# A long convolution by FFT with a routed MLP: padded input blocks, a wider last stage and a reordered first transform

## The chip, the cores and the metric

One Trainium2 chip, one core of it. The metric is the device time of one launch in microseconds (us). Engines: PE multiplies matrices, DVE (VectorE), ACT (ScalarE) and POOL (GpSimd) work on vectors, SP issues most transfers. The kernel before takes 1100.68 us, the median of 3 runs (1099.55 to 1101.87).

## The reference

The convolution of x (8 batches, 6336 positions, 128 channels) with h along the sequence, then for each batch an MLP on the 128 positions with the highest score:

```python
def _attn_ref(x, h):
    L = 2 * S
    Xf = np.fft.rfft(x, n=L, axis=1)
    Hf = np.fft.rfft(h, n=L, axis=0)
    y = np.fft.irfft(Xf * Hf[None, :, :], n=L, axis=1)[:, :S, :]
    return y

def _moe_ref(x, w_gate, w1, w2, capacity):
    scores = np.einsum('bsd,d->bs', x, w_gate)
    out = x.copy()
    for b in range(B):
        top_idx = np.argpartition(-scores[b], capacity)[:capacity]
        xe = x[b, top_idx]
        ye = np.maximum(xe @ w1, 0.0) @ w2
        g = 1.0 / (1.0 + np.exp(-scores[b, top_idx]))
        out[b, top_idx] = x[b, top_idx] + g[:, None] * ye
    return out
```

All inputs are float32; capacity is 128.

## The kernel before, in words

The sequence is written as 99 n1 by 64 n2 (6336 = 99 x 64). Two batches are worked on at once, so there are four groups g. For one group and one half of the channels (u is 0 or 1) the work has four stages.

- **stage_a** transforms over n1. The host lays the input out folded around the middle of n1 (`_lay`), in eight blocks of eight channels. `load` (L83) brings a block into one of two slots of the big tile `slots`, 64 + 50 = 114 partitions by 1024 numbers. `turn` (L158) makes the sum and the difference of its halves on DVE (tile `xs`, L164), up to three blocks ahead. For each block PE then makes two units of matmuls (L186), and each unit's PSUM tile is emptied by ACT, one in eight by DVE (L190, through the helper at L67 and L69).
- **stage_b** goes through 25 chunks of up to four k1. `over_n2` (L228) multiplies by a table `wb` (matmuls at L63), lets ACT make a swapped copy in PSUM (L234, L235), multiplies by the spectrum of h on DVE (twice L239) and adds the two products on POOL (L246). Each chunk needs a table and a piece of spectrum, 256 KB each. `stage_first` does the same for the first u of group 0 and makes the spectrum of h on the way, which it stores to `hd`.
- **stage_c** transforms over k2 with the constant table `wc`: 16 units, each 16 matmuls and one copy of 99 x 1024.
- **stage_d** goes over the 64 n2, two per step (`nd` = 2). Four matmuls of 256 columns fill half of a PSUM tile `both` of 1024 columns that two steps share; ACT copies the half to `hr` (L283) and issues the output DMA (L285); POOL multiplies by `w_gate` (L288; DVE does it for the last step of the last two pairs), and DVE reduces to scores (L291). Its tables come in pairs of n2, half of them into `hr`.

The selection of the 128 positions (`pick`) is one generator with 26 steps of small DVE operations and small matmuls, and the MLP (`feed`) another; `mix` (L485) takes a step of the side work after every so many steps of the main work, at given rates. The schedule is manual: each engine runs its instructions in the order in which the code issues them. In group 0 the order is four units of stage_c, then stage_a for x's second half with one unit of stage_c after every fourth, then the second stage_b. In later groups both halves of stage_a come first, with the selection of the group before at rate 0.1, then both stage_b, the second with stage_c of the first half beside it. The eight loads of a half of x are issued one after another on SP; those of group 0's second half go out in the last eight chunks of stage_first. PSUM has four tiles of 1024 columns, used in turn. The tag `t` of six tiles serves `xs`, the products `tx` and the gated copy `tm`.

## Time and profile before

| | |
|---|---|
| median of 3 runs | 1100.68 us |
| profiled execution, its own time | 1103.47 us |
| its span | 1101.7 us |
| PE busy | 919.0 us (83%) |
| DVE busy | 653.4 us (59%) |
| ACT busy | 566.3 us (51%) |
| POOL busy | 427.3 us (39%) |
| DMA | 194.75 MB, 177 GB/s mean over the span |

The profile is of one execution. Its busy shares are means over stages that differ in what limits them, and PE's busy time is modelled, since matmuls are pipelined. Matmuls of float32 stand as two instructions each in the trace. The granted clock is that of PE as a share of 2.4 GHz; 0.50 is the lower of its two levels, 1.2 GHz.

### The profile page before, as it was taken

To read this page: it belongs to the slowest core of one execution; us is meant where nothing else is said; L and a number is where in the kernel's file an instruction comes from. 1 tells how busy PE (TensorE), PEld (TensorE's weight loads), DVE (VectorE), ACT (ScalarE), POOL (GpSimd) and SP (SyncE) were. 2 spreads that over 40 slices of the span, in tenths; PEclk is the share of its full clock that TensorE was granted. 3 is DMA by queue.
4 is the path that set the end of the run, shared out by engine and by line. 5 is a ranking of instruction groups with operands and counts; after the bars stand their busy time and mean duration, and the time that the engine had idled before them with its cause. 6 is when DMAs were issued, how large, how long until landed. Compare 5 with 4: busy or idle time off the path is not lost.

```text
span 1101.7 us, 34992 instructions
## 1 busy us (share of the span) xinstructions
PE 919.0 (83%) x14710; PEld 787.8 (72%) x14710; DVE 653.4 (59%) x1250; ACT 566.3 (51%) x845; POOL 427.3 (39%) x340
## 2 busy tenths in 40 slices
PE   6899798788878799988878799988868799888765
PEld 5699787775567589865577699855667699755544
DVE  3456556402365879644576878735667787544573
ACT  4477576542247777532277676522466776422101
POOL 0034315405530875035504765045406853055301
PEclk9799999998998999999999899999999999999888
DMA  3578659665536996425458885345368972055100
GB/s 146 178 236 255 226 151 245 198 192 178 162 121 215 335 306 194 156 84 159 129 177 266 276 284 173 112 123 162 123 203 274 307 252 78 14 158 152 57 5 10
DMA packets 115195, 194.75 MB, mean 177 GB/s; under 512 B 11344, under 2 KB 54224, under 8 KB 115040
## 3 DMA queue, kind: packets, MB, share of 16 engines
q1 hardware_dynamic: 87776, 165.52, 47.4%
q10 hardware_dynamic: 26752, 25.96, 7.1%
q8 instruction: 117, 1.92, 0.7%
q0 software_dynamic: 512, 1.05, 0.3%
q14 instruction: 38, 0.31, 0.1%
HBM read 156.27 MB, written 39.45 MB: 178 GB/s over the span
## 4 chain that ended last, share of the span: by engine, by line
PE 42%; DVE 9%; issue 5%; DMA 5%; ACT 4%; POOL 4%; SPq 0%; POOLq 0%; ACTq 0%; DVEq 0%
PE p L63 25%; PE p L279 10%; PE p L186 4%; DMA w<-tab_wb 4%; POOL tm L288 3%; ACT hr L283 2%; DVE tx L239 1%; DVE cmp L321 1%; DVE num L324 1%; DVE xs L164 1%; PE m L63 1%; ACT p L234 1%; DVE sc L291 1%; ACT p L235 1%; DVE slots L239 1%
## 5 line engine op out<-in xcount | busy, mean ns | idle before, releaser
L246 POOL TENSOR_TENSOR slots<-slots,tx 128x512 f32<-128x512 f32 (+1 forms) x200 | 255.7, 1298 | 344.1 <-DVE tx L239 256.5
L67 ACT COPY slots<-p 99x1024 f32<-99x1024 f32 (+3 forms) x266 | 247.7, 935 | 166.1 <-PE p L63 86.5
L63 PE MATMUL p<-wc,slots 128*64 128x128 f32 (+1 forms) x4096 | 248.0, 276 | 9.9 <-POOL slots L246 8.9
L288 POOL TENSOR_TENSOR tm<-hr,wg 99x512 f32<-99x512 f32 x120 | 155.4, 1299 | 255.8 <-ACT hr L283 199.6
L63 PEld LDWEIGHTS p<-wc,slots 128*64 128x64 f32 (+1 forms) x4096 | 229.5, 127 | 13.5 <-POOL slots L246 10.2
L63 PE MATMUL p<-slots,w 128*64 128x128 f32 (+1 forms) x2900 | 200.6, 283 | 40.2 <-DMA w<-tab_wb 19.5
L63 PEld LDWEIGHTS p<-slots,w 128*64 128x64 f32 x2900 | 172.9, 138 | 55.9 <-ACT p L235 35.1
L291 DVE TENSOR_REDUCE sc<-tm 99x4 f32<-99x512 f32 x128 | 87.5, 685 | 207.5 <-POOL tm L288 207.2
L283 ACT COPY hr<-p 99x512 f32<-99x512 f32 x128 | 74.9, 585 | 222.9 <-PE p L279 175.1
L279 PE MATMUL p<-slots,hr 99*99 99x256 f32 x512 | 128.3, 391 | 50.0 <-ACT hr L283 50.0
L186 PE MATMUL p<-fx,xs 50*64 50x99 f32 x4608 | 133.2, 266 | 43.1 <-issue 22.5
L186 PEld LDWEIGHTS p<-fx,xs 50*64 50x64 f32 x4608 | 119.8, 146 | 56.7 <-issue 29.3
L239 DVE TENSOR_TENSOR slots<-p,hr 128x512 f32<-128x512 f32 (+1 forms) x175 | 119.3, 682 | 63.2 <-ACT p L235 61.6
L279 PEld LDWEIGHTS p<-slots,hr 99*99 99x99 f32 x512 | 79.4, 165 | 98.5 <-ACT hr L283 77.3
L234 ACT ACTIVATE p<-p 64x512 f32<-64x512 f32 (+1 forms) x200 | 113.1, 566 | 56.8 <-PE p L63 47.0
L279 PE MATMUL p<-slots,w 99*99 99x256 f32 x512 | 123.0, 381 | 4.6 <-ACT slots L67 4.6
L164 DVE TENSOR_TENSOR xs<-slots 114x512 f32<-114x512 f32 x144 | 94.3, 707 | 50.0 <-PE p L186 26.2
L239 DVE TENSOR_TENSOR tx<-p,hr 128x512 f32<-128x512 f32 (+1 forms) x175 | 118.0, 674 | 0.0
L235 ACT COPY p<-p 64x512 f32<-64x512 f32 (+1 forms) x200 | 110.8, 554 | 6.3
L279 PEld LDWEIGHTS p<-slots,w 99*99 99x99 f32 x512 | 82.8, 164 | 32.1 <-ACT slots L67 5.6
L69 DVE COPY slots<-p 99x1024 f32<-99x1024 f32 (+2 forms) x54 | 48.8, 904 | 34.6 <-ACT slots L67 25.7
L63 PE MATMUL p<-slots 128*64 128x64 f32 (+1 forms) x664 | 47.1, 249 | 3.5 <-ACT p L234 3.5
(90 smaller groups left out, 516.1 us busy)
## 6 DMA issues: line engine op xcount, KB each, us to landing
w<-tab_wb SPq DMA_DIRECT2D x172, 256.0 KB
hr<-hd SPq DMA_DIRECT2D x144, 256.0 KB
slots<-in_x SPq DMA_DIRECT2D x64, 456.0 KB
out<-hr ACTq DMA_DIRECT2D x128, 198.0 KB
w<-tab_at SPq DMA_DIRECT2D x64, 153.1 KB
hr<-tab_at SPq DMA_DIRECT2D x64, 153.1 KB
hr<-hd SPq DMA_DIRECT2D x48, 128.0 KB
slots<-tab_wb SPq DMA_DIRECT2D x20, 256.0 KB
```

Of the source, the lines that this page charges most:

```text
L63: nc.tensor.matmul(out[a:b], table[:, a:b], moving, start=start, stop=stop)
L67: nc.scalar.copy(out=dst, in_=src)
L164: v.tensor_tensor(out=xt[0:HX].rearrange("p d n -> p (d n)"), in0=flat[0:HX, o:o + XB // 2], in1=flat[0:HX, o + XB // 2:o + XB], op=op)
L186: nc.tensor.matmul(pt[c * 64:(c + 1) * 64, o:o + N1], xt[c][e, q * 4 + j], fx[e, c * N1:(c + 1) * N1], start=True, stop=True)
L234: nc.scalar.mul(out=pw[0:64], in_=pv[64:128], mul=-1.0)
L235: nc.scalar.copy(out=pw[64:128], in_=pv[0:64])
L239: v.tensor_tensor(out=dst, in0=src.rearrange("p k (b j t) -> p k b j t", b=2, t=2), in1=ht[:, t, 0:kn].rearrange("p k (j t) -> p k j t", t ...
L246: adds.tensor_tensor(out=yv, in0=yv, in1=tx.rearrange("p k (j t) -> p k j t", t=2), op=ALU.add)
L279: nc.tensor.matmul(pt[0:N1, i * 2 * D:(i + 1) * 2 * D], at[:, i % 2, c], zp[:, :, c * N2 + m], start=(c == 0), stop=(c == 1))
L283: nc.scalar.copy(out=yt.rearrange("p b n (u d) -> p (n u) b d", u=2), in_=pt[0:N1, 0:512].rearrange("p (n b d) -> p n b d", b=nb, d=HD))
L288: (v if m0 in (N2 - 6, N2 - 2) else nc.gpsimd).tensor_tensor(out=tm, in0=hr[0:N1, o:o + 512].rearrange("p (c d) -> p c d", d=D), in1=wg[0: ...
L291: v.tensor_reduce(out=ss[:, :, m0:m0 + nd], in_=tm.rearrange("p (b n) d -> p b n d", b=nb), axis=AX.X, op=ALU.add)
```

## The change

Four things. The host no longer cuts the zero rows off the input, and `load` brings 128 partitions instead of 114; `turn` still reads 114. stage_d takes four n2 per step: each step has a PSUM tile of its own, one ACT copy and one output DMA of twice the size, and the gating product and its reduction go batch by batch, each still of 512 numbers; DVE multiplies the second batch of the last two steps. In groups 1 to 3 the second half of stage_a stands beside the first stage_b, 0.7 of its units after each chunk, and the MLP's rate there is 0.36 instead of 0.4; the selection is taken along at rate 0.1 in the first half of stage_a only. In group 0 four units of stage_a come ahead of all of stage_c, then one unit of stage_c after every second, and x's second half is requested four chunks earlier in stage_first.

```diff
     def load(src, u, blocks=range(8)):
         for i in blocks:
-            nc.sync.dma_start(out=flat[0:HX, u * XS + i * XB:u * XS + (i + 1) * XB], in_=src[i])
+            nc.sync.dma_start(out=flat[:, u * XS + i * XB:u * XS + (i + 1) * XB], in_=src[i])
...
-        nb, nd = 2, 2
+        nb, nd = 2, 4
...
-            if m0 % (2 * nd) == 0:
-                both = banks()
-            pt = both[:, m0 % (2 * nd) * 2 * D:]
+            pt = banks()[0:N1]
...
-            o = m0 // nd % 4 * 512
-            yt = hr[0:N1, o:o + 512].rearrange("p (b n d) -> p b n d", b=nb, d=D)
+            o = m0 // nd % 2 * 1024
+            yt = hr[0:N1, o:o + 1024].rearrange("p (b n d) -> p b n d", b=nb, d=D)
             nc.scalar.copy(out=yt.rearrange("p b n (u d) -> p (n u) b d", u=2),
-                           in_=pt[0:N1, 0:512].rearrange("p (n b d) -> p n b d", b=nb, d=HD))
+                           in_=pt.rearrange("p (n b d) -> p n b d", b=nb, d=HD))
             nc.scalar.dma_start(out=ov[:, :, m0:m0 + nd], in_=yt)
-            tm = tp.tile([N1, 4, D], F32, tag="t", name="tm", bufs=6)
-
-            (v if m0 in (N2 - 6, N2 - 2) else nc.gpsimd).tensor_tensor(
-                out=tm, in0=hr[0:N1, o:o + 512].rearrange("p (c d) -> p c d", d=D),
-                in1=wg[0:N1].unsqueeze(1).broadcast_to([N1, 4, D]), op=ALU.mult)
-            v.tensor_reduce(out=ss[:, :, m0:m0 + nd], in_=tm.rearrange("p (b n) d -> p b n d", b=nb),
-                            axis=AX.X, op=ALU.add)
-            if m0 % (2 * nd):
-                yield
+            for b in range(nb):
+                tm = tp.tile([N1, nd, D], F32, tag="t", name="tm", bufs=6)
+
+                (v if b and m0 >= N2 - 2 * nd else nc.gpsimd).tensor_tensor(
+                    out=tm, in0=yt[:, b], in1=wg[0:N1].unsqueeze(1).broadcast_to([N1, nd, D]), op=ALU.mult)
+                v.tensor_reduce(out=ss[:, b, m0:m0 + nd], in_=tm, axis=AX.X, op=ALU.add)
+            yield
...
     for i, _ in enumerate(stage_first()):
-        if i >= NK - 8:
-            load(x[0, 1], 0, [i - NK + 8])
+        if NK - 12 <= i < NK - 4:
+            load(x[0, 1], 0, [i - NK + 12])
...
         if g:
-            mix(itertools.chain(stage_a(0, 0, [(1, 0), (1, 8)]), stage_a(1, D)), (side, 0.1))
-            mix(stage_b(g, 0), (iter(()) if g < 2 else fed.pop(0), 0.4))
+            mix(stage_a(0, 0, [(1, 0), (1, 8)]), (side, 0.1))
+            a = stage_a(1, D)
+            mix(stage_b(g, 0), (iter(()) if g < 2 else fed.pop(0), 0.36), (a, 0.7))
+            rest(a)
         else:
-            mix(itertools.islice(c, 4))
-            mix(stage_a(0, D), (c, 0.25))
+            a = stage_a(0, D)
+            rest(itertools.islice(a, 4))
+            mix(a, (c, 0.5))
...
-    r = r.reshape(a.shape[:-5] + (128, XB))
-    return r[..., :HX, :]
+    return r.reshape(a.shape[:-5] + (128, XB))
```

The order of the instructions on PE in stage_d, with what each waits for (DMAHW is a landing, Activation is ACT, PE is PE itself). Before, a step of two n2 takes one table, `w` or `hr` in turn:

```order
L279 MATMUL p<-slots,w 99x256 [waits DMAHW6_49,PE_49]
L279 MATMUL p<-slots,w 99x256 x3
L279 MATMUL p<-slots,hr 99x256 [waits DMAHW0_49,Activation_49]
L279 MATMUL p<-slots,hr 99x256 x3
L279 MATMUL p<-slots,w 99x256 [waits DMAHW2_49,PE_49]
L279 MATMUL p<-slots,w 99x256 x3
L279 MATMUL p<-slots,hr 99x256 [waits DMAHW4_49,Activation_49]
L279 MATMUL p<-slots,hr 99x256 x3
```

and of the change:

```order
L277 MATMUL p<-slots,w 99x256 [waits DMAHW4_49,Activation_49]
L277 MATMUL p<-slots,w 99x256 x3
L277 MATMUL p<-slots,hr 99x256 [waits DMAHW5_49]
L277 MATMUL p<-slots,hr 99x256 x3
L277 MATMUL p<-slots,w 99x256 [waits DMAHW7_49,Activation_49]
L277 MATMUL p<-slots,w 99x256 x3
L277 MATMUL p<-slots,hr 99x256 [waits DMAHW0_49]
L277 MATMUL p<-slots,hr 99x256 x3
```

The wait for ACT has moved from the second half of four n2, whose PSUM tile ACT is reading at that time, to the first, where it is for the copy of the tile that was filled four tiles earlier.

PE from the end of stage_d in group 0 on, with L186 stage_a (16 matmuls a unit), L63 from `slots,w` the first products over n2 (8 matmuls a chunk). Before:

```order
L279 MATMUL p<-slots,hr 99x256 x4
L186 MATMUL p<-fx,xs 64x99 x512
L63 MATMUL p<-slots,w 64x128 x238
L63 MATMUL p<-wc,slots 64x128
L63 MATMUL p<-wc,slots 35x128
```

and of the change:

```order
L277 MATMUL p<-slots,hr 99x256 x4
L186 MATMUL p<-fx,xs 64x99 x256
L63 MATMUL p<-slots,w 64x128 x16
L186 MATMUL p<-fx,xs 64x99 x16
L63 MATMUL p<-slots,w 64x128 x8
L186 MATMUL p<-fx,xs 64x99 x16
L63 MATMUL p<-slots,w 64x128 x16
L186 MATMUL p<-fx,xs 64x99 x16
```

The second 256 matmuls of stage_a now come in units of 16 behind every first or second chunk.

DVE at the end of stage_d in group 1, where L408 and L404 (`hit`) and what follows are the last operations of the selection of group 0, L392 and L388 its lane operations, L164 the turns for group 2. Before:

```order
L394 SCALAR_TENSOR_TENSOR cmp<-tri,first,cmp 99x128
L291 TENSOR_REDUCE sc<-tm 99x2x2 x4
L408 TENSOR_SCALAR hit<-m,cst 128x256
...
L291 TENSOR_REDUCE sc<-tm 99x2x2 x2
L164 TENSOR_TENSOR xs<-slots 114x512 x4
L291 TENSOR_REDUCE sc<-tm 99x2x2 x3
L288 TENSOR_TENSOR tm<-hr,wg 99x512
L291 TENSOR_REDUCE sc<-tm 99x2x2 x2
L288 TENSOR_TENSOR tm<-hr,wg 99x512
L291 TENSOR_REDUCE sc<-tm 99x2x2
L164 TENSOR_TENSOR xs<-slots 114x512 x8
```

and of the change:

```order
L164 TENSOR_TENSOR xs<-slots 114x512 x4
L289 TENSOR_REDUCE sc<-tm 99x4 x3
L287 TENSOR_TENSOR tm<-hr,wg 99x512
L289 TENSOR_REDUCE sc<-tm 99x4
L388 TENSOR_SCALAR cmp<-tri,last 99x128
L390 SCALAR_TENSOR_TENSOR cmp<-tri,first,cmp 99x128
L388 TENSOR_SCALAR cmp<-tri,last 99x128
L390 SCALAR_TENSOR_TENSOR cmp<-tri,first,cmp 99x128
L289 TENSOR_REDUCE sc<-tm 99x4
L287 TENSOR_TENSOR tm<-hr,wg 99x512
L289 TENSOR_REDUCE sc<-tm 99x4
L404 TENSOR_SCALAR hit<-m,cst 128x256
```

The selection, which ended before the turns of the next group's first two blocks, now ends behind the last reduction; the turns of the third block come after it.

## Rows read from the trace of the kernel before

**Rows 1.** Timeline of the opening: start us, us, engine, line, operation, idle before and releaser.
```profile
6.51 1.29 DVE L164 TENSOR_TENSOR xs<-slots 114x512 f32<-114x512 f32 x2 [5.50 <-DMA slots<-in_h]
9.47 1.29 DVE L164 TENSOR_TENSOR xs<-slots 114x512 f32<-114x512 f32 x2 [1.67 <-DMA slots<-in_h]
...
40.09 3.42 PE L186 MATMUL p<-fx,xs 50*64 50x99 f32 x64 [0.90 <-DVE xs L164]
...
57.17 0.46 PE L207 MATMUL p<-slots,w 128*64 128x64 f32 x8
```

**Rows 2.** Busy time by stretch: stretch, its us, engines, granted clock, DMA share, GB/s.
```profile
8.00:20.00 12.00, 10.89 (x263) 9.65 (x267) 5.17 (x8) 6.22 (x7) 0.00 (x0) 1.00 0.40 161
40.00:57.00 17.00, 16.00 (x319) 14.30 (x320) 6.61 (x10) 7.29 (x9) 0.00 (x0) 0.50 0.60 193
316.00:351.00 35.00, 26.93 (x1026) 24.83 (x1024) 23.20 (x40) 25.57 (x29) 0.00 (x0) 0.94 0.55 184
351.00:395.00 44.00, 32.97 (x463) 27.39 (x462) 34.86 (x55) 31.43 (x57) 32.74 (x26) 0.97 0.94 319
740.00:760.00 20.00, 17.12 (x77) 11.68 (x78) 9.04 (x14) 4.68 (x8) 11.33 (x9) 1.00 0.54 159
791.00:826.00 35.00, 25.03 (x1015) 23.00 (x1017) 24.22 (x41) 25.42 (x29) 0.93 (x1) 0.98 0.57 186
826.00:876.00 50.00, 40.08 (x606) 36.14 (x600) 38.63 (x66) 34.74 (x65) 35.11 (x29) 0.94 0.86 285
```

The engines in these rows are PE, PE's weight loads, DVE, ACT and POOL.

**Rows 3.** Timeline of PE in stage_a of group 3.
```profile
794.72 1.74 PE L186 MATMUL p<-fx,xs 50*64 50x99 f32 x47 [0.50 <-DVE xs L164]
...
800.98 2.95 PE L186 MATMUL p<-fx,xs 50*64 50x99 f32 x127 [1.36 <-issue]
...
805.31 2.95 PE L186 MATMUL p<-fx,xs 50*64 50x99 f32 x127 [1.39 <-issue]
```

**Rows 4.** Timeline of one step of four n2 in stage_d of group 2.
```profile
758.05 1.98 PE L279 MATMUL p<-slots,hr 99*99 99x256 f32 x8 [0.72 <-ACT hr L283]
...
761.84 0.59 ACT L283 COPY hr<-p 99x512 f32<-99x512 f32 x1 [1.15 <-PE p L279]
762.08 0.69 DVE L291 TENSOR_REDUCE sc<-tm 99x4 f32<-99x512 f32 x1 [1.08 <-POOL tm L288]
...
762.48 1.98 PE L279 MATMUL p<-slots,hr 99*99 99x256 f32 x8 [0.72 <-ACT hr L283]
762.51 1.27 POOL L288 TENSOR_TENSOR tm<-hr,wg 99x512 f32<-99x512 f32 x1 [0.46 <-ACT hr L283]
```

**Rows 5.** PE's waits in stage_d, group 0, then each later group: us, times, longest.
```profile
PE p L279 <- ACT hr L283: 15.7, 16, 5.0
```
```profile
PE p L279 <- ACT hr L283: 11.4, 16, 0.7
```

**Rows 6.** Timeline of PE behind stage_first.
```profile
125.65 8.57 PE L63 MATMUL p<-wc,slots 128*35 128x128 f32 x126 [4.54 <-POOL slots L246]
```

**Rows 7.** Timeline of DVE in stage_d, group 2, and at the end of group 3's.
```profile
767.11 1.18 DVE L392 TENSOR_SCALAR cmp<-tri,last 99x128 bf16<-99x128 f32 x1
...
768.91 0.35 DVE L394 SCALAR_TENSOR_TENSOR cmp<-tri,first,cmp 99x128 bf16<-99x128 f32 x1
...
775.97 0.47 DVE L408 TENSOR_SCALAR hit<-m,cst 128x256 f32<-128x256 f32 x1
...
777.72 0.16 DVE L419 TENSOR_TENSOR iu<-ge,thr 128x1 uint32<-128x1 f32 x1
...
1032.12 0.69 DVE L288 TENSOR_TENSOR tm<-hr,wg 99x512 f32<-99x512 f32 x1 [0.66 <-ACT hr L283]
```

**Rows 8.** Timeline of DVE and POOL where both read SBUF.
```profile
539.59 5.41 POOL L288 TENSOR_TENSOR tm<-hr,wg 99x512 f32<-99x512 f32 x4
...
542.72 4.03 DVE L164 TENSOR_TENSOR xs<-slots 114x512 f32<-114x512 f32 x4
...
851.18 2.05 DVE L447 TENSOR_TENSOR slots<-xe,wg 128x128 f32<-128x128 f32 x1
```

More of the change, by code (lines that the diff above doesn't have):

```diff
@@ L278, in stage_d @@
                 for c in range(2):
-                    nc.tensor.matmul(pt[0:N1, i * 2 * D:(i + 1) * 2 * D], at[:, i % 2, c], zp[:, :, c * N2 + m],
+                    nc.tensor.matmul(pt[:, i * 2 * D:(i + 1) * 2 * D], at[:, i % 2, c], zp[:, :, c * N2 + m],
                                      start=(c == 0), stop=(c == 1))
-            o = m0 // nd % 4 * 512
-            yt = hr[0:N1, o:o + 512].rearrange("p (b n d) -> p b n d", b=nb, d=D)
+            o = m0 // nd % 2 * 1024
+            yt = hr[0:N1, o:o + 1024].rearrange("p (b n d) -> p b n d", b=nb, d=D)
             nc.scalar.copy(out=yt.rearrange("p b n (u d) -> p (n u) b d", u=2),
-                           in_=pt[0:N1, 0:512].rearrange("p (n b d) -> p n b d", b=nb, d=HD))
+                           in_=pt.rearrange("p (n b d) -> p n b d", b=nb, d=HD))
             nc.scalar.dma_start(out=ov[:, :, m0:m0 + nd], in_=yt)
-            tm = tp.tile([N1, 4, D], F32, tag="t", name="tm", bufs=6)
-            (v if m0 in (N2 - 6, N2 - 2) else nc.gpsimd).tensor_tensor(
-                out=tm, in0=hr[0:N1, o:o + 512].rearrange("p (c d) -> p c d", d=D),
-                in1=wg[0:N1].unsqueeze(1).broadcast_to([N1, 4, D]), op=ALU.mult)
-            v.tensor_reduce(out=ss[:, :, m0:m0 + nd], in_=tm.rearrange("p (b n) d -> p b n d", b=nb),
-                            axis=AX.X, op=ALU.add)
-            if m0 % (2 * nd):
-                yield
+            for b in range(nb):
[4 more added lines that the diff above has]
+            yield
     def pick(b0, nb, ss, new):
```

## The prediction

> **What bounds the kernel now.** I read the busy time by stretch first, to cut the span into stages, then the timeline of each stage that the diff touches, then who waited for whom there. The sum is made against the profiled execution, which took 1103.5 us; the median of the three timed runs is 1100.7, so 2.8 us come off at the end.
>
> Four places matter. In the opening, DVE gets a block of input about every 2.97 us and stands still before each one, waiting for the load [rows 1]; the DMA engines meanwhile show a share of 0.40 with one queue of loads running [rows 2], as if 6.4 of 16 engines carried them. Each load has 114 partitions; the tables with 128 partitions that fill the stretch 351 to 395 reach 0.94 and 319 GB/s [rows 2], 339 GB/s at full share. Where loads don't limit, stage_a moves at 4.33 us for two blocks, and PE's idle time before each pair is put down to issue [rows 3]. In stage_d, PE works through four n2 in two halves of one PSUM tile and stops 0.72 us before each four, until ACT has emptied the half just filled [rows 4]; that is 11.4 us in each of three groups and 15.7 us in the first [rows 5]. Between them, stage_a (35 us) and the first products over n2 (44 to 50 us) follow one another [rows 2]: the first leaves POOL idle and DMA at 0.55, the second has DMA at 0.86 to 0.94 and PE at three quarters to four fifths.
>
> **The change part by part.** *Padded loads.* 72 loads grow by 14 rows of 4 KB, 4.1 MB in all; at 339 GB/s that is 12 us of transfer over the whole span, beside other work, and I cost it at nothing after the opening. A block becomes 524 KB, 1.55 us at 339 GB/s. In the opening the pace per block is then the largest of 1.55 (load), 1.29 (DVE, [rows 1]) and half of 4.33, which is 2.17 (PE's issue, [rows 3]). I take 2.1, between this and the 35 us for 16 blocks of a later stage_a [rows 2]. Sixteen blocks make 33.6 us, from a first block at about 5 us, against an end at 57.2 [rows 1]: **minus 18.5**. Bounds: at the load's 1.55 us, minus 27. At the other end PE stays at 1.2 GHz, the granted 0.50 of 40 to 57 us [rows 2], where 64 matmuls, one block, took 3.42 us [rows 1]: 16 of them end at 60 us, plus 3. I take the nearer to stage_a's own pace, since there the clock was granted at 0.94 to 0.98 at a like density [rows 2].
>
> *C behind four units, x earlier.* In group 0 PE waited 4.54 us for POOL's last sums before the first unit of C [rows 6]. Three blocks of stage_a now stand there, 4.5 us of PE at 2.95 us a pair [rows 3], so the wait is covered if x has landed; its eight loads leave four chunks earlier. **Minus 4.5**; 0 if x is late. Those loads run beside stage_first's stores, and SP takes each between two stores and the next table. I cost it at nothing, since tables are requested six chunks ahead; with that cover gone it is 8 x 1.55 = 12.4 us.
>
> *stage_d, four n2 at a time.* Each four has its own PSUM tile and one ACT copy, so the wait on the copy of the same tile goes: 16 a group, 3 x 11.4 + 15.7, **minus 49.9** [rows 5]. The step is then PE's own, 4.43 - 0.72 = 3.71 us. Under it lie one copy of twice the size (two of 0.59, at most 1.2), two POOL products of 1.27 [rows 4], two reductions of 0.69 on DVE [rows 4], and one output DMA in place of two, of the same bytes. All fit in 3.71, POOL at 2.54 the nearest. The bound at the other end is a step that stays at 4.43, gain 0.
>
> *The end of stage_d.* The copy is later by half a tile, and only the second half of the last two steps is multiplied on DVE. After PE's last but one step DVE is done about 1.0 (copy) + 1.27 (POOL) + 3 x 0.69 (a reduction, a product, a reduction) = 4.3 us later; as the selection now runs two steps behind (stage_a feeds it once, not three times), four lane operations follow (767.11 to 769.26, 2.15 us [rows 7]), and PE waits for them before stage_a: 6.5 - 3.7 = 2.8 us. After the last step DVE still has its reductions and seven selection operations (775.97 to 777.88, 1.9 us [rows 7]), then the turn of the third block, 1.29. That ends 11.2 us after the same point, while PE has two turned blocks, 2.95 us, until 9.5: 1.7 more. Less the 0.50 that this start costs now [rows 3], 4 us for each of two groups; 2.6 for the one without a selection (8.0 + 1.29 on DVE against 3.7 + 2.95 on PE). In the tail the last scores and that selection end 6.2 us after PE, where 0.59 + 2 x 0.69 = 2.0 us stand now: 4.2. Together **plus 15**; 5 if DVE's work overlaps better, 20 with every piece late.
>
> *Half of stage_a beside the first products.* Half of 35 us plus 44 is 61.5 us in group 1, half of 35 plus 50 is 67.5 in group 3 [rows 2], group 2 the same. Merged, the engines' own sums (half of stage_a plus the second stretch) are in group 1 PE 46.4, DVE 46.5, ACT 44.2, POOL 32.7, and DMA 0.94 x 44 = 41; in group 3 PE 52.6, DVE 50.7, ACT 47.5 [rows 2]. If that were all, the gains are 13 to 15 us a group, 39 to 45 in sum. But stage_a's turns (L164, two operands in SBUF) have run without POOL; now POOL adds beside them. Beside POOL's products of stage_d four took 4.03 us [rows 8] against 2 x 1.29 [rows 1], and in the products' stretch a smaller operation on two SBUF operands took 2.05 us [rows 8], 1.4 more than a turn. I price a pair of turns at 1.3 us extra, eight pairs a group, 10.4: DVE 57 and 61, stages of 58 and 62. Gains 3.5, 5 and 5.5: **minus 14**. Bounds: minus 40 with no such cost; with 1.4 for each of 16 turns, DVE 69 and 73, plus 18.
>
> The Trainium skill, SBUF — State Buffer, "Who interferes with whom", says that a VectorE operation with two SBUF inputs and a GpSimd one that reads SBUF exclude each other for a whole instruction. That speaks against this merge: the two long rows above would be no accident but the price of every turn that meets a POOL sum. By the rule, as an estimate with half of a 1.27 us POOL operation for each of 16 turns, the merge brings about 14 us; by the engines' sums alone it brings 40.
>
> The sum: -18.5 - 4.5 - 49.9 + 15 - 14 = -71.9, so 1031.6 as profiled and **1029** against the median. With the likely parts of the bounds (opening -23 to -12, stage_d -50 to -40, merge -25 to -3) this case runs from 1012 to 1047.
>
> **The rivals.** *The merge runs at the engines' sums* (POOL's operations leave gaps enough): another 26 us, 1003. For it: POOL is idle a quarter of that stretch; against it: [rows 8]. Chance 0.18.
>
> *The merge costs more than it hides.* DVE waits on POOL at every turn, and with DVE's queue in order the products behind it hold PSUM tiles that PE needs: plus 18 instead of minus 14, 1061. For it: in group 1 the sums of PE, DVE and ACT lie within 3 us of one another. Chance 0.09.
>
> *stage_d finds another limit* and stays at 4.43: 1029 + 50 = 1079. The share of 0.54 there [rows 2] would rise to 0.64 at 3.71 us, far from 0.94, so I give it 0.07 rather than less only for the longer hold of each output buffer. The Trainium skill, DMA: Bandwidth & Descriptors, "Why a DMA increments its semaphore by 16 and not by 1", would have transfers of 99 partitions on 11 engines of 16, an estimate of 0.69 as their ceiling; no run here shows it, and 0.64 would stand just under it.
>
> *The padding does not spread the loads*: blocks come at 2.97 x 128/114 = 3.34 us, the opening ends 6 us later, 1029 + 18.5 + 6 = 1053; chance 0.04, since 128-partition tables reach 0.94. *The opening runs at 1.2 GHz*: 1029 + 21.5 = 1050; chance 0.04.
>
> *Slower than before.* Interleaved units leave PE more and shorter stops, and the granted clock falls to half in the merged stages. The PE sums of 46.4, 52.6 and 52.6 us would double; in place of 58 + 62 + 62 they take 303, plus 121: 1150. It decides against the change once three fifths of that time is at 1.2 GHz (72 of 121). For it: 0.50 was granted in 40 to 57 us, after PE had waited on loads. Against: 0.94 to 0.98 in all stages concerned. Chance 0.02.
>
> **How the numbers follow.** My own case has 0.56. A measurement of this kernel can tell about 0.2% from no change, 2 us. Only the last rival is slower, and the far ends of the others come nowhere near no change: faster 0.97, same 0.01, slower 0.02. The range takes in my case, the gainful merge down to 1003 and the two openings at 1050 to 1053, and leaves out the dearer merge, the unchanged stage_d and the slow clock, 0.18 in all: 1000 to 1055.
>
> **What would show it.** Right: stage_first's first matmul at about 38 us with a DMA share near 0.9 before; no PE wait for ACT's copy in stage_d and a step of 3.7 us; a PE wait of about 3 us for the lane operations at the end of stage_d; L164 at a mean well over its 0.65 us in the merged stretch, and that stretch at 58 to 62 us. Wrong: a stage_d step above 4 us, a granted clock of one half in any merged stage, or an opening past 45 us.

## The result, and the profile after

The changed kernel takes 1038.8 us, the median of 4 runs (1036.6 to 1042.1), against 1100.1 for the kernel before (4 runs): a ratio of 0.945, 95% interval 0.941 to 0.949. The forecast was 1029, with a range of 1000 to 1055. The profiled execution took 1042.1 us (span 1040.3), so 61.4 us of 1103.5 went; the forecast sum was 71.9. Cut at PE's first matmul of each stage, the span reads:

| stage, us | before | after | difference | forecast |
|---|---|---|---|---|
| opening, to stage_first | 57.2 | 44.5 | -12.7 | -18.5 |
| group 0, stage_first to stage_d | 181.2 | 179.9 | -1.3 | -4.5 |
| stage_d, groups 0, 1, 2 | 77.8, 72.2, 72.2 | 55.6, 61.5, 61.5 | -43.6 | with the next row |
| stage_d of group 3 and the tail | 142.5 | 133.2 | -9.3 | -34.9 for both |
| stage_a and first products, groups 1 to 3 | 80.3, 86.7, 86.2 | 82.3, 89.4, 89.1 | +7.6 | -14 |
| second products and stage_c, groups 1 to 3 | 81.8 each | 81.2, 81.5, 80.6 | -2.1 | 0 |

The row of stage_a and the first products runs to PE's first matmul of stage_c, so it takes in the first three chunks of the second products. stage_d gave 18 us more than forecast; the opening, group 0 and the merge gave less, and the merge, which was to gain 14 us, lost 7.6. The two upper rows vary from run to run: in ten later runs with the padded opening it took 44.5 to 47.4 us, and in seven with the same code up to stage_d group 0 took 177.2 to 181.2.

**stage_d.** The timeline of PE in group 1:

```profile
482.72 1.90 PE L277 MATMUL p<-slots,w 99*99 99x256 f32 x8
484.46 1.89 PE L277 MATMUL p<-slots,hr 99*99 99x256 f32 x8
486.19 1.90 PE L277 MATMUL p<-slots,w 99*99 99x256 f32 x8
```

No idle time stands before a row, where half of the rows had 0.72 us for ACT before [rows 4]. Four n2 take 3.47 us (482.72 to 486.19), not the 3.71 that were forecast. The wait of [rows 5] is gone. What PE still waits for ACT in stage_d is 0.9 to 1.1 us a group, for the last copy of stage_c, and that stood there before too, with 1.1 to 1.2 us.

**The end of stage_d and the first half of stage_a**, PE in group 1 and on into group 2:

```profile
500.10 0.22 PE L402 MATMUL m<-hf,cmp 99*128 99x64 bf16 x2
504.15 0.19 PE L400 MATMUL m<-lane,cmp 99*128 99x1 bf16 x1 [3.83 <-DVE cmp L390]
...
504.98 7.85 PE L186 MATMUL p<-fx,xs 50*64 50x99 f32 x223
513.71 2.97 PE L186 MATMUL p<-fx,xs 50*64 50x99 f32 x127 [0.88 <-issue]
520.33 5.44 PE L186 MATMUL p<-fx,xs 50*64 50x99 f32 x162 [3.65 <-issue]
```

PE stops for the selection's lane operations, as forecast (3.8 us for 2.8). Then 223 matmuls take 7.85 us and 162 take 5.44, where 127 take 2.97 at the full clock: at that pace they would be 5.2 and 3.8, so 4.3 us are lost to the clock (0.50 from 505 to 510 us and 0.66 from 520 to 525, in the rows of the last section), and 3.65 us to a stop put down to issue.

**The stages by engine.** Busy time by stretch: for each group first the half of stage_a that stands alone, then the merged stretch (stretch, its us, PE, PE's weight loads, DVE, ACT, POOL, granted clock, DMA share, GB/s):

```profile
280.00:304.00 24.00, 16.31 (x515) 15.23 (x514) 16.93 (x30) 13.57 (x15) 1.42 (x2) 0.76 0.87 318
304.00:362.30 58.30, 48.63 (x988) 42.04 (x990) 48.41 (x72) 44.54 (x72) 35.34 (x28) 0.92 0.77 242
505.00:527.10 22.10, 16.24 (x513) 15.66 (x512) 16.43 (x34) 12.52 (x14) 2.90 (x2) 0.79 0.77 296
527.10:594.40 67.30, 57.09 (x1118) 49.75 (x1120) 51.55 (x82) 47.21 (x80) 38.26 (x31) 0.91 0.69 216
737.40:759.80 22.40, 16.35 (x514) 15.56 (x512) 16.46 (x34) 12.54 (x14) 2.92 (x2) 0.80 0.78 294
759.80:826.50 66.70, 56.92 (x1119) 49.80 (x1121) 50.02 (x82) 47.36 (x80) 37.81 (x30) 0.92 0.69 212
```

The half that was counted as 17.5 us takes 24.0, 22.1 and 22.4 at a granted clock of 0.76 to 0.80; the merged stretches take 58.3, 67.3 and 66.7 where 58, 62 and 62 were forecast. DVE's turns in the three of them (groups by line: busy us, mean ns, idle before), and in the second one pair of turns with the sums beside it, and one turn that came behind a sum:

```profile
L164 DVE TENSOR_TENSOR xs<-slots 114x512 f32<-114x512 f32 x12 | 12.3, 1050 | 3.5 <-POOL slots L246 3.5
L164 DVE TENSOR_TENSOR xs<-slots 114x512 f32<-114x512 f32 x12 | 12.2, 1046 | 3.5 <-POOL slots L246 3.5
L164 DVE TENSOR_TENSOR xs<-slots 114x512 f32<-114x512 f32 x12 | 11.2, 955 | 4.4 <-POOL slots L246 4.4
```

```profile
548.00 2.56 POOL L246 TENSOR_TENSOR slots<-slots,tx 128x512 f32<-128x512 f32 x2 [1.70 <-DVE tx L239]
549.33 2.38 DVE L164 TENSOR_TENSOR xs<-slots 114x512 f32<-114x512 f32 x2 [0.28 <-POOL slots L246]
572.19 0.69 DVE L164 TENSOR_TENSOR xs<-slots 114x512 f32<-114x512 f32 x1 [1.18 <-POOL slots L246]
```

A turn takes 1.05, 1.05 and 0.96 us in the mean, against 0.65 alone [rows 1]. The mean hides two kinds: 11 of the 36 turns begin just behind the start of a sum and take 1.76 to 1.80 us, as the first of the pair at 549.33 does, and the other 25 take 0.68. Besides, DVE stands idle for a sum to end ahead of 18 of them, 11.4 us in all.

**The opening**, PE, and the busy time of its two halves:

```profile
5.89 8.51 PE L186 MATMUL p<-fx,xs 50*64 50x99 f32 x222 [5.89 <-DVE xs L164]
15.22 2.95 PE L186 MATMUL p<-fx,xs 50*64 50x99 f32 x127 [0.81 <-issue]
21.56 4.42 PE L186 MATMUL p<-fx,xs 50*64 50x99 f32 x127 [3.39 <-issue]
28.12 11.15 PE L186 MATMUL p<-fx,xs 50*64 50x99 f32 x381 [2.14 <-issue]
```

```profile
0.00:20.00 20.00, 11.46 (x349) 10.77 (x349) 11.25 (x18) 9.31 (x10) 0.20 (x4) 1.00 0.92 353
20.00:40.00 20.00, 15.81 (x520) 15.10 (x524) 10.23 (x17) 11.30 (x13) 0.00 (x0) 0.74 0.53 185
```

The loads run at a share of 0.92 and 353 GB/s against 0.40 and 161 [rows 2], and they are no longer what PE waits for. It is held by stops put down to issue and by the clock (0.74 from 20 to 40 us).

**Group 0**, the end of stage_first, on PE and on DVE:

```profile
114.74 0.41 PE L186 MATMUL p<-fx,xs 50*64 50x99 f32 x4 [4.14 <-DVE xs L164]
```

```profile
112.97 0.56 DVE L239 TENSOR_TENSOR slots<-p,w1s 128x384 f32<-128x384 f32 x1 [1.35 <-ACT p L235]
113.45 0.55 DVE L239 TENSOR_TENSOR tx<-p,w1s 128x384 f32<-128x384 f32 x1
113.91 4.50 DVE L164 TENSOR_TENSOR xs<-slots 114x512 f32<-114x512 f32 x6
```

The wait of 4.54 us for POOL's last sums [rows 6] is gone, and one of 4.14 us stands in its place: x had landed, but the turns stand in DVE's queue behind the products of the last chunk, which wait for ACT.

### The profile page after: what moved, and what is told of

It reads as the page before. It is cut to its first block, busy times and chain, and to the rows that moved or that the text cites. A ratio compares the mean times of both kernels' runs of the same rounds, so it can differ in the third digit from the quotient of the medians.

```text
span 1040.3 us, 34561 instructions
## 1 busy us (share of the span) xinstructions
PE 909.1 (87%) x14707; PEld 798.9 (77%) x14707; DVE 648.2 (62%) x1250; ACT 554.5 (53%) x781; POOL 436.1 (42%) x340
## 3 DMA queue, kind: packets, MB, share of 16 engines
q0 software_dynamic: 512, 1.05, 0.3%
## 5 line engine op out<-in xcount | busy, mean ns | idle before, releaser
L246 POOL TENSOR_TENSOR slots<-slots,tx 128x512 f32<-128x512 f32 (+1 forms) x200 | 259.4, 1312 | 316.4 <-DVE tx L239 273.5
L67 ACT COPY slots<-p 128x792 f32<-128x792 f32 (+3 forms) x266 | 248.3, 938 | 163.1 <-PE p L63 78.7
L63 PE MATMUL p<-wc,slots 128*64 128x128 f32 (+1 forms) x4096 | 246.2, 275 | 2.7 <-POOL slots L246 2.6
L287 POOL TENSOR_TENSOR tm<-hr,wg 99x512 f32<-99x512 f32 x120 | 158.8, 1344 | 210.5 <-issue 151.2
L63 PEld LDWEIGHTS p<-wc,slots 128*64 128x64 f32 (+1 forms) x4096 | 228.6, 127 | 4.9 <-POOL slots L246 3.7
L63 PE MATMUL p<-slots,w 128*64 128x128 f32 (+1 forms) x2900 | 201.7, 284 | 28.7 <-DMA w<-tab_wb 9.3
L63 PEld LDWEIGHTS p<-slots,w 128*64 128x64 f32 x2900 | 172.0, 139 | 42.2 <-ACT p L234 8.7
L186 PE MATMUL p<-fx,xs 50*64 50x99 f32 x4608 | 142.3, 281 | 43.8 <-issue 20.5
L186 PEld LDWEIGHTS p<-fx,xs 50*64 50x64 f32 x4608 | 127.0, 157 | 59.4 <-issue 32.2
L281 ACT COPY hr<-p 99x1024 f32<-99x1024 f32 x64 | 64.8, 1013 | 165.7 <-PE p L277 133.2
L164 DVE TENSOR_TENSOR xs<-slots 114x512 f32<-114x512 f32 x144 | 104.7, 774 | 29.8 <-PE p L186 13.3
L277 PE MATMUL p<-slots,hr 99*99 99x256 f32 x512 | 121.1, 377 | 0.0
L277 PEld LDWEIGHTS p<-slots,hr 99*99 99x99 f32 x512 | 83.4, 163 | 27.5
L69 DVE COPY slots<-p 99x1024 f32<-99x1024 f32 (+2 forms) x54 | 48.7, 902 | 35.5 <-ACT slots L67 20.4
L63 PE MATMUL p<-slots 128*64 128x64 f32 (+1 forms) x664 | 46.6, 249 | 2.3 <-ACT p L234 2.3
```

Source lines behind the costliest of these rows:

```text
L63: nc.tensor.matmul(out[a:b], table[:, a:b], moving, start=start, stop=stop)
L67: nc.scalar.copy(out=dst, in_=src)
L164: v.tensor_tensor(out=xt[0:HX].rearrange("p d n -> p (d n)"), in0=flat[0:HX, o:o + XB // 2], in1=flat[0:HX, o + XB // 2:o + XB], op=op)
L186: nc.tensor.matmul(pt[c * 64:(c + 1) * 64, o:o + N1], xt[c][e, q * 4 + j], fx[e, c * N1:(c + 1) * N1], start=True, stop=True)
L246: adds.tensor_tensor(out=yv, in0=yv, in1=tx.rearrange("p k (j t) -> p k j t", t=2), op=ALU.add)
L277: nc.tensor.matmul(pt[:, i * 2 * D:(i + 1) * 2 * D], at[:, i % 2, c], zp[:, :, c * N2 + m], start=(c == 0), stop=(c == 1))
```

## The experiments

Three questions were open: why the first half of stage_a is slow, what the merge costs, and whether the stop for the selection is worth removing. The runs in one table (medians, and ratios to the kernel before as timed beside the run; stages in us, to about 0.1, each from one profiled execution; A is stage_a with the first products in groups 1, 2, 3, cut as above):

| kernel | us | ratio, 95% | opening | stage_d, groups 0 to 2 | A |
|---|---|---|---|---|---|
| changed | 1038.8 | 0.941-0.949 | 44.5 | 55.6, 61.5, 61.5 | 82.3, 89.4, 89.1 |
| stage_d alone | 1051.4 | 0.951-0.962 | 56.4 | 57.2, 57.7, 57.7 | 80.8, 83.6, 90.4 |
| padding alone | 1089.0 | 0.981-0.997 | 46.4 | 70.9, 72.1, 72.1 | 83.9, 86.6, 88.1 |
| no merge | 1034.2 | 0.936-0.948 | 47.4 | 55.6, 57.7, 57.7 | 83.8, 88.1, 86.1 |
| selection early | 1039.1 | 0.938-0.947 | 44.8 | 55.6, 57.7, 57.7 | 82.3, 92.9, 92.2 |
| no padding | 1078.8 | 0.975-0.983 | 57.6 | 63.4, 61.5, 61.5 | 91.5, 94.8, 93.0 |
| loads later | 1041.8 | 0.943-0.951 | 47.0 | 55.7, 61.5, 61.5 | 82.4, 88.7, 88.7 |
| no POOL sums | 1019.9 | 0.922-0.929 | 44.5 | 55.7, 61.5, 61.4 | 76.7, 82.0, 80.9 |
| no merge, loads later | 1035.7 | 0.937-0.944 | 46.2 | 55.6, 57.5, 56.9 | 84.1, 87.6, 90.4 |
| no merge, x in stage_c | 1029.0 | 0.931-0.941 | 45.3 | 57.9, 57.8, 57.7 | 77.4, 84.5, 84.4 |
| the same, turns early | 1020.9 | 0.921-0.934 | 45.3 | 61.1, 57.7, 57.6 | 77.4, 83.6, 85.1 |
| no merge, turns early | 1029.3 | 0.931-0.939 | 45.5 | 55.6, 57.7, 57.6 | 82.0, 87.4, 87.7 |
| merge, turns early | 1035.5 | 0.936-0.944 | 45.0 | 55.6, 57.7, 57.7 | 83.1, 90.9, 89.9 |

**stage_d alone.** The edit is the changed `stage_d` in the kernel before.

> The kernel before with the changed stage_d alone. In the changed kernel the step of four n2 fell from 4.43 to 3.47 us. Theory (the step's gain is stage_d's own, and PE's 3.8 us wait for the selection at the end of a stage_d arises because fewer selection steps stand ahead of it): here three selection steps stay in stage_a, the wait is small, and the time is about 55 to 60 us below the kernel before, near 1043. Rival (the wait belongs to the wide step itself): the wait stays at 3 to 4 us and the gain is 45 to 50 us, near 1052.

1051.4 us, the median of four runs from 1046.3 to 1058.9, some 8 us above the theory's figure and 1 us below the rival's. By the time the rival has it; the profiled execution, with a span 57 us below that of the kernel before, was the fastest of the four. But the theory's signs are there: PE's wait for the lane operations sums to 2.4 us over the kernel, longest 0.7, and a stage_d of groups 1 and 2 takes 57.7 us where it takes 61.5 in the changed kernel. The stop has only moved: in groups 2 and 3 it stands before the third block's turn, with 5.4 and 5.2 us.

```profile
516.28 2.97 PE L186 MATMUL p<-fx,xs 50*64 50x99 f32 x128
524.62 5.62 PE L186 MATMUL p<-fx,xs 50*64 50x99 f32 x128 [5.37 <-DVE xs L164]
```

**Padding alone.** The kernel before with this edit, and with the zero rows kept on the host:

```diff
-            nc.sync.dma_start(out=flat[0:HX, u * XS + i * XB:u * XS + (i + 1) * XB], in_=src[i])
+            nc.sync.dma_start(out=flat[:, u * XS + i * XB:u * XS + (i + 1) * XB], in_=src[i])
...
```

> The kernel before with the padded loads alone. Theory (eight padded loads at a DMA share near 1.0 hold up the stage_a that starts beside them, by starving PE's instruction loading and through the clock that falls after the stops): the opening gains about 12.7 us, each of the three later stage_a loses 3 to 5 us, net -3 us or so, near 1097. Rival (the slow stage_a of the changed kernel comes from elsewhere): -12 to -13 us, near 1088, later stage_a at 35 us as before.

1089.0 us, nearer to the rival's 1088, but the four runs spread from 1083.3 to 1099.1, so the profile has to tell. The opening gained 10.8 us; a stage_a takes 36.5 to 36.9 us against 35.0 to 35.5 before, at a clock of 0.86 in all three groups against 0.94 to 0.98 [rows 2]:

```profile
537.00:573.90 36.90, 29.66 (x1025) 27.32 (x1024) 23.93 (x41) 24.15 (x28) 0.73 (x1) 0.86 0.55 201
```

So padded loads do slow the stage_a beside them, but by 1 to 2 us, not 3 to 5.

**No padding in the changed kernel**, the reverse edit there.

> The changed kernel with the loads of before (114 partitions, DMA share 0.40). Theory (the loads at full share starve PE's instruction loading): PE's waits put down to issue in the first half of stage_a fall from 3.3 to 3.7 us to 1.5 or less, that half takes 18 to 20 us in place of 22 to 24, about -10 us over three groups, and the opening gives back 12.7: near 1041. Rival (that half is slow because DVE's turns come late behind the scores and the selection): it stays at 22 us and more, and the whole is near 1051.

1078.8 us, 40 us above the changed kernel and beyond both expectations. The opening gives 13.1 us back; the rest is new. At a DMA share of 0.40 the eight loads of x's second half hold the queue so long that the tables behind them come late:

```profile
335.35 3.68 PE L63 MATMUL p<-slots,w 128*64 128x128 f32 x32 [13.78 <-DMA w<-tab_wb]
```

That is 13.8 us in group 1, 8.4 and 10.8 in the next two, and in stage_d of group 0 a table is 4.3 us late. In the kernel before the first products came 35 us after these loads, and hid them; the merge brings them forward by half of stage_a. So the padding is worth 11 to 14 us alone and 40 us under the merge. The theory fails on its own sign too: with the loads at their old pace PE's longest stop for issue in the first half of stage_a was still 3.2, 2.6 and 1.3 us, against 3.3, 3.7 and 3.7 in the changed kernel.

**Selection early.**

```diff
-            mix(stage_a(0, 0, [(1, 0), (1, 8)]), (side, 0.1))
+            mix(stage_a(0, 0, [(1, 0), (1, 8)]), (side, 0.2))
```

> The changed kernel with the selection taken along at rate 0.2 in place of 0.1 in the first half of stage_a: three steps there in place of one, so that the selection ends two steps earlier in the next stage_d. Theory (PE's waits of 3.8 us for the lane operations at the end of stage_d in groups 1 and 2, and the clock of one half that follows, come from these two steps): the wait goes in two groups, -7 to -12 us, near 1029. Rival (DVE is behind there anyway, with the last scores): the wait moves to the turns or the scores, -2 us or less.

1039.1 us: the rival. The stop of 3.8 us at the end of stage_d went (57.7 for 61.5 us), and A grew by 3.5 and 3.1 us, since PE now stops for the third block's turn. DVE, and PE, at that place:

```profile
509.01 0.69 DVE L289 TENSOR_REDUCE sc<-tm 99x4 f32<-99x512 f32 x1 [0.45 <-POOL tm L287]
509.61 0.68 DVE L287 TENSOR_TENSOR tm<-hr,wg 99x512 f32<-99x512 f32 x1
510.33 0.69 DVE L289 TENSOR_REDUCE sc<-tm 99x4 f32<-99x512 f32 x1
510.93 3.69 DVE L164 TENSOR_TENSOR xs<-slots 114x512 f32<-114x512 f32 x6
```

```profile
511.76 7.06 PE L186 MATMUL p<-fx,xs 50*64 50x99 f32 x219 [5.39 <-DVE xs L164]
```

The turns of L164 begin when the last score is reduced. DVE's and POOL's chain of scores is late at this seam, whatever stands before it.

**No merge.**

```diff
-            mix(stage_a(0, 0, [(1, 0), (1, 8)]), (side, 0.1))
-            a = stage_a(1, D)
-            mix(stage_b(g, 0), (iter(()) if g < 2 else fed.pop(0), 0.36), (a, 0.7))
-            rest(a)
+            mix(itertools.chain(stage_a(0, 0, [(1, 0), (1, 8)]), stage_a(1, D)), (side, 0.1))
+            mix(stage_b(g, 0), (iter(()) if g < 2 else fed.pop(0), 0.4))
```

> The changed kernel with both halves of stage_a one after the other ahead of the first products, as before (and the selection and MLP rates of before with them). Theory (the merge gains a little, 2 to 5 us a group, and the slow first half of stage_a comes from the padded loads): this kernel keeps the slow first half, loses the merge's gain, and gets back the 3.8 us waits for the selection in two groups: within 5 us of the changed kernel, 1035 to 1043. Rival (the merge itself is what costs the 7.6 us over these stages): stages of 80, 87 and 86 us as before, 1022 to 1028.

1034.2 us, 1 us under the theory's range and 6 above the rival's, and the slow stage_a is kept (37.1, 38.8 and 36.5 us, against 35.0 to 35.5 before). But the merge is not the small gain that the theory had. By the median the kernel without it is 4.6 us faster than the changed one, though the intervals overlap. "Selection early" differs from this kernel little but in the merge, and its A is 1.5 us shorter in group 1 and 4.8 and 6.1 longer in groups 2 and 3: a loss of 9.4 in sum.

**No POOL sums in the merged stretch.**

```diff
-        adds.tensor_tensor(out=yv, in0=yv, in1=tx.rearrange("p k (j t) -> p k j t", t=2), op=ALU.add)
+        adds and adds.tensor_tensor(out=yv, in0=yv, in1=tx.rearrange("p k (j t) -> p k j t", t=2), op=ALU.add)
...
-            mix(stage_b(g, 0), (iter(()) if g < 2 else fed.pop(0), 0.36), (a, 0.7))
+            mix(stage_b(g, 0, (None,)), (iter(()) if g < 2 else fed.pop(0), 0.36), (a, 0.7))
```

> The changed kernel without POOL's additions of the two products in the merged stretch of groups 1 to 3 (a part of the computation is left out: there only the first product is kept). Theory (turns on DVE and sums on POOL exclude each other, and this is what the merge loses): the turns fall back to 0.65 us each, DVE no longer waits for POOL, the merged stretches take 52, 60 and 60 us in place of 58, 67 and 66: -15 to -20, near 1021. Rival (PE, at the granted clock of 0.92 and with its own stops for ACT and DVE, sets these stretches): -5 us or less.

1019.9 us, 19 below the changed kernel, and the three stretches as expected, 52.1, 59.5 and 58.3 us:

```profile
305.10:357.20 52.10, 47.11 (x988) 40.65 (x990) 43.42 (x71) 44.21 (x72) 2.33 (x2) 0.95 0.83 270
521.90:581.40 59.50, 54.17 (x1120) 46.84 (x1122) 46.49 (x82) 46.78 (x80) 4.83 (x5) 0.97 0.76 239
745.90:804.20 58.30, 52.66 (x1118) 45.39 (x1120) 46.25 (x81) 46.79 (x80) 4.69 (x5) 1.00 0.77 242
```

```profile
L164 DVE TENSOR_TENSOR xs<-slots 114x512 f32<-114x512 f32 x12 | 7.7, 683 | 0.0
```

A turn is back at 0.68 us and waits for nobody. POOL's sums cost the merged stretches 6.2, 7.8 and 8.4 us, 22.4 in all, part of it by the clock, which was 0.91 to 0.92 with them and 0.95 to 1.00 without; without them A is 4 to 5 us a group shorter than in the kernel before. It is the turns beside them that make the sums dear: in the kernel without the merge neither PE nor DVE waits for a sum in these stretches.

The run takes away two things at once. The longer turns are 12.0 us of DVE's time over the three groups (means of 1050, 1046 and 955 ns for 683, 12 turns each), and its idle time ahead of turns is 11.4. That idle time is a wait for tiles, as far as trace and code tell: both turns of a pair wait for POOL, and with three blocks turned ahead, of two tiles each, all six tiles `t` hold turned blocks, so a pair needs the two tiles of the last two products and can't begin before these are summed. By this the second turn of the pair at 549.33 would have waited for the second sum, until 550.56, even if the first had taken 0.68 us. More tiles `t` would tell what the slow turns cost by themselves; no such run was made.

**Loads later, with and without the merge.** Each of the eight loads of x's second half is issued ahead of two units of stage_a, not at the end of stage_d:

```diff
+            wide = stage_a(0, 0, [(1, 0), (1, 8)])
+            for i in range(8):
+                load(x[g, 1], 1, [i])
+                rest(itertools.islice(wide, 2))
...
-            load(x[g + 1, 1], 1)
```

> The changed kernel with the eight loads of the second half of x issued one by one, each ahead of two units of the first half of stage_a, in place of all eight at the end of stage_d. Theory (loads at full share starve PE's instruction loading): the issue waits fall to 1.5 us or less, the first half of stage_a takes 18 to 20 us, -8 to -12 us in sum, near 1029. Rival (DVE's turns are what is late there): -3 us or less, and PE waits for DVE's turns instead.

> The changed kernel with stage_a and the first products one after the other as before, and the eight loads of the second half of x issued one by one ahead of two units of stage_a each; the selection takes its three steps in stage_a. Theory (loads at full share starve PE's instruction loading): stage_a takes 34 to 35 us in place of the 36.5 to 38.8 us of the variant without the merge, -6 to -10 us against that variant, near 1026. Rival (DVE's late turns): within 2 us of that variant, 1032 to 1036.

1041.8 and 1035.7 us, no gain in either. They don't decide what they were made for: SP waits for nothing between these loads, and sent all eight in one go, 4 us after the seam between groups 1 and 2 with the merge (shown here) and 10 us after it without.

```profile
508.89 5.20 SPq L85 DMA_DIRECT2D slots<-in_x  x8
```

The loads were moved, not thinned out, and the issue stops stayed at up to 3.4 us.

**x's second half loaded in stage_c.** The variant without the merge, with these loads where the DMA share was 0.31:

```diff
         ahead(("at", g, 0), True)
+        if not last:
+            load(x[g + 1, 1], 1)
...
-            load(x[g + 1, 1], 1)
```

> The variant without the merge (1034.2), with the eight loads of the second half of x requested before the second half of stage_c, where the DMA share is 0.31, in place of at the end of stage_d. Theory (loads at full share beside stage_a hold up PE's instruction loading): PE's issue waits in stage_a fall from 18.7 us to about 9, and each stage_a is 2 to 3 us shorter: near 1026. Rival (PE stops for DVE's late turns, and the clock that is granted after the stop is the cost): the issue waits may fall, the stop of 5 to 6 us at each turn and the clock of 0.82 stay, and the time is within 3 us of that variant, 1031 to 1037.

Here x's blocks overwrite part of what stage_c stores, since both lie in the tile `slots`, so stage_d works on other numbers: this shows what the loads cost, and it shows why they stand where they do. 1029.0 us against 1034.2, with overlapping intervals; by the profiles the three stages A are 11.7 us shorter in sum, 8.6 of them in stage_a. stage_a of group 1 without the merge, first with the loads beside it, then without, and PE's waits in the same stretches:

```profile
280.80:317.90 37.10, 30.21 (x1025) 28.07 (x1024) 25.48 (x43) 24.48 (x28) 1.38 (x2) 0.82 0.56 207
```

```profile
284.60:317.10 32.50, 26.56 (x1027) 24.76 (x1026) 25.05 (x43) 25.87 (x29) 1.38 (x2) 0.95 0.27 83
```

```profile
PE p L186 <- issue: 4.3, 2, 2.2
```

```profile
PE p L186 <- issue: 3.4, 5, 1.1
```

The sum of the issue waits hardly falls, but the long ones go (longest 1.1, 0.9 and 0.9 us in the three groups, for 2.2, 2.6 and 1.5) and the clock stays at 0.95 in group 1. In groups 2 and 3, where PE still stops 5.3 us for the turn, the clock is 0.86 and 0.90 and stage_a takes 35.9 and 35.4. Each theory has its part in this pair: with x's loads beside it stage_a has longer issue stops, DVE's late turn makes another, and the clock is lower where there is either.

**The first turns early**, on top of that variant, and then alone, with and without the merge:

```diff
-        mix(itertools.islice(d, 13), (side, 0.5))
-        if not last:
-            turn((0, 0))
-            turn((0, 8))
+        for n, o in ((10, 0), (3, 8), (2, 16)):
+            mix(itertools.islice(d, n), (side, 0.5))
+            if not last:
+                turn((0, o))
         mix(d, (side, 0.5))
```

> As the kernel with the second half of x loaded in stage_c, and the turns of the first three blocks issued after steps 10, 13 and 15 of stage_d, in place of two after step 13 and the third behind all scores. Theory (the DVE chain of two turns beside POOL and then the last scores, the third turn behind them, is what PE stops for at the end of stage_d, and the clock falls behind the stop): PE's stops for DVE's turns fall from about 23 us in sum to under 5, the granted clock in stage_a is 0.92 or more, each stage_a takes 34 to 35 us: 8 to 14 us below the kernel without the early turns, near 1015 to 1020. Rival (with six tiles the earlier turns take tiles from POOL's products, and the stop moves to the scores or to the fourth turn): within 3 us of it.

> The variant without the merge (1034.2), with x's loads where the changed kernel has them and the first three turns after steps 10, 13 and 15 of stage_d. Theory (PE's stop for the third turn costs a stage_a its length and the clock behind it): the stop falls from 5.4 to 2.8 us as in the variant with the loads in stage_c, stage_a takes 35 to 37 us, -4 to -8 us, near 1028. Rival (with the loads beside it stage_a waits as long for instructions instead): within 2 us of 1034.

> The changed kernel with both: the selection at rate 0.2, and the first three turns after steps 10, 13 and 15 of stage_d, the merge kept; beside it runs the same without the merge. Theory (the merge brings a loss because of the lock between turns and sums, 6 to 8 us in each of three groups): 3 to 8 us above the kernel without the merge, near 1033. Rival (the merge only lost by PE's late start of it): at or below that kernel, near 1027 or less.

The first (x in stage_c, so again with other numbers in stage_d) took 1020.9 us for 1029.0, and the second 1029.3 for 1034.2, near the theories' figures, but the intervals overlap, and by the profiles the spans differ by only 1.2 and 1.7 us: the gain is not settled. (In the first, stage_a fell from 35.9 and 35.4 to 34.0 and 33.9 us in groups 2 and 3, while stage_d of group 0 grew from 57.9 to 61.1.) The stop for the third turn fell from 5.3 to 2.8 us,

```profile
506.99 10.94 PE L186 MATMUL p<-fx,xs 50*64 50x99 f32 x335 [2.80 <-DVE xs L164]
```

and is not gone, because the fourth block's turns and the last scores still share DVE. Where x's loads are beside it, the stage_a takes 37.1, 37.9 and 37.0 us at clocks of 0.82, 0.82 and 0.86, no less than the 37.1, 38.8 and 36.5 without the early turns: there the rival holds. The pair with and without the merge, run beside each other, goes the theory's way: 1035.5 against 1029.3, within its 3 to 8 us, A longer by 6.8 us in sum. The two intervals overlap a little (0.936 to 0.944 and 0.931 to 0.939), but it is the fourth such pair: by their medians the kernels with the merge were 4.6 (changed), 4.9 (selection early), 6.0 (loads later) and 6.2 us slower than their counterparts without it.

The version without the merge and with early turns is the fastest that computes the reference: 1029.3 us, ratio 0.935 (0.931 to 0.939), an interval below that of the changed kernel (0.941 to 0.949).

## Why the prediction was right, and where it was off

- *The whole* came 10 us slower than forecast, inside the range. It came this near by luck: one term's surplus (stage_d, 18 us) made up for most of the others' shortfall (opening 5.8, group 0 3.2, merge 21.6). Two of its own signs of being right failed, the first matmul of stage_first at about 38 us (44.5) and the merged stretch at 58 to 62 us (58.3, 67.3 and 66.7). And the ends that it names for its own case add up to 1013 and 1056, not to 1012 and 1047.
- *stage_d and its end*, -34.9 forecast, -52.9 measured. The mechanism was right: the wait for the copy of the same tile went. Two sizes were off. The step became 3.47 us, not 4.43 - 0.72 = 3.71: a run of eight matmuls takes 1.74 us from start to start when nothing stops between them, so each stop had cost about 0.2 us more than its idle time shows. Over 64 steps that is 15 of the 18 us. And "4 us for each of two groups" at the end came out for another reason: the selection's stop, put at 2.8, took 3.8, while the further 1.7 for the third turn didn't appear; it appears, at 5.2 to 5.4 us, as soon as the selection is out of the way.
- *The opening*, -18.5 forecast, -12.7 measured. The loads spread as forecast. The step that failed is the pace of 2.1 us a block, "nearer to stage_a's own pace, since there the clock was granted at 0.94 to 0.98": sixteen blocks took 38.6 us, 2.4 each. (2.1 is also less than both rates between which it is said to lie, 2.17 and 35 / 16 = 2.19.) PE's stops for issue, 7.2 us, were no longer than in a later stage_a of the kernel before (5.9 to 9.3); its matmuls were slower. At 2.95 us for 127 those of the rows at 5.89, 21.56 and 28.12 would take 17.0 us, not 24.1. Of these 7 us 3.8 lie behind 20 us, where the clock was granted at 0.74: the rival of an opening at 1.2 GHz came in part. The other 3.4 lie in the row at 5.89, where the profile shows a granted clock of 1.00 and matmuls came at about half their pace all the same (88 in 4.10 us from 5 to 10 us); why stays open.
- *Group 0*, -4.5 forecast, -1.3 measured (0 to -4 by the later runs). "Covered if x has landed" asked only about the load. DVE's queue was left out: the turn stands behind the last chunk's products.
- *Padded loads after the opening*, "cost at nothing". Alone this is off by 1 to 2 us a stage_a, at the lower clock. In the changed kernel it is off the other way, and much more: without padding the tables for the merged stretch come 8 to 14 us late, so padding is what lets the merge stand at all.
- *The merge*, -14 forecast, +7.6 measured; the sign failed. The term was built from three sizes. What POOL's sums cost was priced at 10.4 us a group and measured at 7.5, but not as the lock alone that the prediction had: the turns themselves grew by 4.0 us a group, and the waits for tiles ahead of them, which it left out, were 3.8. The Trainium skill, SBUF — State Buffer, "Who interferes with whom", says that a VectorE operation with two SBUF inputs contends with a GpSimd one that reads SBUF; the trace agrees, with 1.76 to 1.80 us for the 11 turns that began inside a sum and 0.68 for the others. The estimate worked out from that rule, half of a 1.27 us POOL operation a turn, was about twice too high: 12.0 us over 36 turns are 0.33 us a turn. The floor under it, "the engines' own sums", was too low: without POOL's sums the stretches took 52.1, 59.5 and 58.3 us against sums of 46.5, 52.6 and 52.6, 18 us in all; there PE, ACT and DVE still wait for one another in turn. And the first half of stage_a was taken as 17.5 us, half of 35; it took 22 to 24, 16 us in all, because alone it lies at the seam, with all of x's loads, the stops and the clock behind them in it. The two shortfalls less the surplus in the price, 25 us, are more than the 21.6 missed by 4 us, since the forecast took these stages before at 79, 85 and 85 us, where they are 80.3, 86.7 and 86.2.
- *The rivals.* "The merge runs at the engines' sums" is excluded, since even without POOL's sums it doesn't. "The merge costs more than it hides" was right in kind (chance 0.09), with 7.6 us in place of 18; of its reason, DVE did wait on POOL, though at half of the turns and not at each. stage_d at 4.43 and loads that don't spread are excluded by the rows above; the DMA share in stage_d rose to 0.62 to 0.63, where 0.64 was forecast. The slow clock came, not in the merged stretches (0.91 and 0.92) but in the half ahead of them (0.76 to 0.80): 4 us in the group read above, where the rival had 121 over three groups.

## What to carry to other kernels

Before merging two stages, list the operations that will newly run beside each other and look for two prices: pairs that hold each other up when they overlap (here turns on DVE and sums on POOL), and a pool of tiles that they share (here the six `t`). And don't take the largest engine's sum as the floor: here a stretch without either took 1.1 times that sum. A stage's mean pace doesn't hold for its first half: what a seam collects (the last scores, the first turns, the next loads) falls on it alone. And a wait that is removed from one engine should be asked for its next holder in every queue, not only in the transfer.

## What the runs showed of the hardware

- Loads with 114 partitions ran at a DMA share of 0.40 and 161 GB/s, and at 0.36 and 139 GB/s in the opening of the run without padding; with 128 they ran at 0.92 and 353. The Trainium skill, DMA: Bandwidth & Descriptors, "Why a DMA increments its semaphore by 16 and not by 1", has a transfer run on the largest number of engines up to 16 that divides the slowest dimension of both sides, which is 16 for 128 partitions and, worked out, 6 for 114, an estimate of 0.375 for the share; these rows agree.
- Behind the long stops of PE shown here the granted clock fell to the lower level for some microseconds, and then stood at 1.00 again. Not every stop of some length did this: one of 2.77 us in the kernel before (it ended at 856.5) and one of 2.35 in the run without padding (307.4) left the clock at 1.00, where one of 2.35 in the changed kernel (285.4) was followed by 0.56 from 285 to 290. Busy time of the changed kernel in stretches of 5 us, from the seam between group 1 and 2 on:

```profile
505.00:510.00 5.00, 5.00 (x123) 5.00 (x126) 4.83 (x13) 2.43 (x3) 1.55 (x1) 0.50 1.01 403
510.00:515.00 5.00, 4.12 (x171) 3.92 (x167) 3.33 (x6) 3.85 (x5) 1.35 (x2) 0.91 1.03 406
515.00:520.00 5.00, 1.68 (x79) 1.48 (x71) 4.70 (x11) 1.78 (x3) 0.00 (x0) 1.00 1.04 381
520.00:525.00 5.00, 4.67 (x140) 4.67 (x144) 2.41 (x4) 3.43 (x4) 0.00 (x0) 0.66 0.31 115
```

  The first follows the stop of 3.83 us, the last the one of 3.65 (520.33). In the kernel before one issue stop of 3.39 us ended at 328.39, and the clock behind it was 0.77:

```profile
331.00:336.00 5.00, 4.74 (x165) 4.54 (x158) 3.04 (x5) 3.85 (x5) 0.00 (x0) 0.77 0.80 217
336.00:341.00 5.00, 3.87 (x168) 3.67 (x171) 2.98 (x6) 4.29 (x6) 0.00 (x0) 1.00 0.65 209
```

  The two stops, ahead of the first half of stage_a in group 2 and within it, cost 7.5 us themselves and 4.3 behind them.
- Stops put down to issue were at most 1.3 us in each of the six stage_a without x's loads beside it. With them they mostly reached 2.0 to 3.8 us, in the kernel before too, but not always: in the run with stage_d alone, with the same unpadded loads beside it as before, the longest were 1.3, 0.9 and 1.0. What makes the long ones is open. That PE's instructions are fetched late is a guess; no run isolates it.
